# Two of four row groups turned by DMA transposes instead of TensorE, in a spectral-mixing kernel with a feed-forward block

## The chip, the cores and the metric

The kernel runs on one core of a Trainium2 chip. The metric is the time of the program on the device in microseconds (us), as the median of several executions. A core has five engines with a program each: TensorE (PE in the profile; its weight loads are PEld), VectorE (DVE), ScalarE (ACT), GpSimd (POOL) and SyncE (SP). SyncE and GpSimd start the transfers of this kernel.

## The reference

A batch of 8 sequences of 3008 rows with 256 columns is filtered in the frequency domain along the rows, and every filtered row goes through a feed-forward block.

```python
def _attn_ref(x, filt_r, filt_i):               # x: (8, 3008, 256)
    X = np.fft.rfft(x, axis=1)
    F = (filt_r + 1j * filt_i)[None, :, :]
    return np.fft.irfft(X * F, n=x.shape[1], axis=1)

def _moe_ref(x, w_in, w_out, beta):             # x: (24064, 256), w_in: (256, 2048)
    h = x @ w_in
    g = h * (1.0 / (1.0 + np.exp(-beta * h)))
    return g @ w_out
```

## The kernel before

The transform of 3008 = 47 x 64 points is done as small matmuls with tables that the kernel makes itself (t1 to t4), in four parts: over the 47, over the 64 (with the filter product), back over the 64, and back over the 47. Between the parts, what lies in columns must come to lie on partitions, so the data is turned twice. Batch 0 is handled on its own in a prologue; for batches 1 to 7 these parts are units of work that are put among the steps of the feed-forward block. A step is one hidden slice of 128 for one block of 512 rows: two hps matmuls of 512 columns, the Silu on ScalarE (to gT), and, two steps later, four acc matmuls of 256 columns.

In batch 0, the third part writes z_t, with J = 32 rows in four groups of JG = 8:

```python
    z_t = ypool.tile([P, NDC, J, KP], BF16, name="z_t", tag="y")     # NDC 2, KP 96
    ...
    def inverse3(i):                       # i: 0 to 11, two of the 24 frequencies each
        ...
        last = i == NK // 2 - 1
        for j0, j1 in ((0, JG), (JG, J)) if last else ((0, J),):
            ...                            # 8 matmuls into ps, then:
            for e in range(2) if last else (None,):
                ...
                evac(dst, src, not last or j0 > 0)     # evac(dst, src, on_act): a copy out of psum
```

and the turn of a row group is done on TensorE, four rows at a time, with the last part behind it:

```python
    def turn_z(g, i, on_act=False):
        ...
        pz = fpsum.tile([P, 4, D], BF16, name="pz", tag="f")
        for e in range(4):
            for dc in range(NDC):
                nc.tensor.transpose(
                    pz[:KP, e, dc * P : (dc + 1) * P], z_t[:, dc, JG * g + 4 * i + e, :], ident[:]
                )
        evac(zz0[g][:, 4 * i : 4 * i + 4, :], pz[:KP], on_act)

    def last_z(g, i, on_act, own=None):    # four matmuls with zz0[g], and a copy into ys[0]
        ...
```

Group 0 is turned in the prologue by a loop of its own (16 transposes); groups 1 to 3 are placed into steps of the feed-forward block. In batches 1 to 7 the first turn is a DMA transpose from SyncE (a2_read: eight transposes of 128x768, two for each of four groups of six frequencies), the second goes through DRAM (d, zz). `place(a, z, units)` spreads units from step a to step z:

```python
    def uz(g, act=False):
        return [lambda i=i: turn_z(g, i) for i in range(2)] + [
            lambda i=i: last_z(g, i, act) for i in range(2 * NDC)
        ]
    ...
    place(1, 14, uz(1, True))
    place(15, 29, uz(2, True))
    units = uz(3, True)
    place(20, 24, units[:2], per=2)
    place(34, 58, units[2:])
    ...
        at = place(9, 14, units[J // 4 :], per=9)                    # the rest of batch 1's first part
        place(at + 1, at + 1, [lambda: a2_read(1)] + uf(JG, NK), per=9)   # uf: loads of filter rows into frr
        ...
        units = u23(1)                                               # batch 1's second and third parts
        place(20, 53, units[: NK // 2], per=2)
    ...
        place(36, 36, ux(2), per=9)                                  # load of batch 2's rows
        at = place(52, 66, u1(2, True), per=3)
```

The last rows are copied out of psum in two halves, by VectorE and ScalarE, into one tile, which one transfer stores:

```python
                    if last and h == nch - 1:
                        for half in range(2):
                            cols = slice(half * P, (half + 1) * P)
                            evac(ost[:, c : c + per, cols], a[:, :, cols], half == 1)
                    else:
                        evac(ost[:, c : c + per, :], a[:], on_act)
                    store(t0 + h * per * P, per * P, ost[:, c : c + per, :])
```

Of the kernel before, what the change touches and what calls it, by code (L numbers as in the profile page):

```python
# [9 lines left out]
P = 128  # L10
# [3 lines left out]
F32 = mybir.dt.float32  # L14
BF16 = mybir.dt.bfloat16
# [24 lines left out]
def kernel(  # L40
# [66 lines left out]
    def evac(dst, src, on_act, scale=None):  # L107
        if on_act:
            nc.scalar.activation(dst, src, ACT.Copy, scale=1.0 if scale is None else scale)  # L109
        elif scale is None:  # L110
            nc.vector.tensor_copy(dst, src)  # L111
        else:
            nc.vector.tensor_scalar_mul(dst, src, scale)  # L113
# [320 lines left out]
    for go in tabs[::-1]:  # L434
        go()

    z_t = ypool.tile([P, NDC, J, KP], BF16, name="z_t", tag="y")
    pq = {}

    def product(i):  # L440
# [22 lines left out]
    def inverse3(i):  # L463
        k0 = 2 * i
        p_t, q_t = pq.pop(i)

        last = i == NK // 2 - 1
        for j0, j1 in ((0, JG), (JG, J)) if last else ((0, J),):
            nj = 4 * (j1 - j0)
            if j0:  # L470
                ps = fpsum.tile([P, 2, NDC, nj], F32, name="psz", tag="f")
            else:
                ps = opsum.tile([P, 2, NDC, nj], F32, name="psz", tag="acc")
            for src, tab in ((p_t, t3), (q_t, t3b)):
                for e in range(2):
                    for dc in range(NDC):
                        nc.tensor.matmul(  # L477
                            ps[:, e, dc, :],
                            lhsT=src[:, e, dc * P : (dc + 1) * P],
                            rhs=tab[:, k0 + e, 4 * j0 : 4 * j1],  # L480
                            start=src is p_t and dc == 0 and e == 0,
                            stop=src is q_t,
                            skip_group_check=True,
                        )
            for e in range(2) if last else (None,):
                if last:
                    dst = z_t[:, :, j0:j1, 4 * (k0 + e) : 4 * (k0 + e) + 4]
                    src = ps[:, e].rearrange("p c (j a) -> p c j a", a=4)
                else:
                    dst = z_t[:, :, :, 4 * k0 : 4 * k0 + 8].rearrange(  # L490
                        "p c j (e a) -> p e (c j) a", e=2
                    )
                    src = ps.rearrange("p e c (j a) -> p e (c j) a", a=4)
                evac(dst, src, not last or j0 > 0)

    def table4():
        for src, dst in ((t1b, t4b), (t1, t4)):
# [39 lines left out]
    ys[0] = ypool.tile([P, NDC, NK * P], BF16, name="y", tag="y")  # L537
    zz0 = {}
    zz0[0] = apool.tile([P, NK * P], BF16, name="zz", tag="a1")
    zz0[0] = zz0[0][:KP, : JG * D].rearrange("p (j d) -> p j d", j=JG)  # L540


    def turn_z(g, i, on_act=False):
        if g not in zz0:
            zz0[g] = zzpool.tile([KP, JG, D], BF16, name="zz", tag="zz")
        pz = fpsum.tile([P, 4, D], BF16, name="pz", tag="f")
        for e in range(4):
            for dc in range(NDC):
                nc.tensor.transpose(  # L549
                    pz[:KP, e, dc * P : (dc + 1) * P], z_t[:, dc, JG * g + 4 * i + e, :], ident[:]  # L550
                )
        evac(zz0[g][:, 4 * i : 4 * i + 4, :], pz[:KP], on_act)

    def last4(zz, tab, jj, dc, dst, on_act, own=None, first=NP):
        ps = own or fpsum.tile([P, 4, P], F32, name="ps4", tag="f")
        for e in range(4):
            nc.tensor.matmul(  # L557
                ps[:, e, :NP],
                lhsT=zz[:, jj + e, dc * P : (dc + 1) * P],
                rhs=tab[:],  # L560
                start=True,
                stop=True,
            )
        rest = []
        for n0, n1 in ((0, NP),) if own is None or first == NP else ((0, first), (first, NP)):
            rest.append(
                lambda n0=n0, n1=n1: evac(
                    dst[:, n0:n1],
                    ps[:, :, n0:n1].rearrange("p j n -> p n j"),
                    on_act,  # L570
                    inv_scale,
                )
            )
        rest.pop(0)()
        return rest

    def last_z(g, i, on_act, own=None):
        jq, dc = divmod(i, NDC)
        c = g * JG // JC + jq
        yv = ys[0][:, dc, c * CLS : (c + 1) * CLS].rearrange("p (n j) -> p n j", j=JC)  # L580

        n0 = NP if jq == 0 else (TB - CLS) // JC
        return last4(zz0[g], t4b, JC * jq, dc, yv, on_act, own, n0)

    for i in range(4):
        if i % 2:
            pz = opsum.tile([P, 2, D], BF16, name="pz", tag="acc")
        else:
            pz = fpsum.tile([P, 2, D], BF16, name="pz", tag="f")
        for e in range(2):  # L590
            for dc in range(NDC):
                nc.tensor.transpose(
                    pz[:KP, e, dc * P : (dc + 1) * P], z_t[:, dc, 2 * i + e, :], ident[:]
                )
        evac(zz0[0][:, 2 * i : 2 * i + 2, :], pz[:KP], i % 2 == 1)
    pw[0] = hpsum.tile([P, TB], F32, name="pw", tag="hps")
    warm(1)
    rest = []
# [40 lines left out]
            on_act,  # L639
        )  # L640

    def a2_read(b):
        s = st[b]
        s["a2"] = []
        for g in range(NG):
            t = a2pool.tile([P, NDC, KG, P], BF16, name="a2", tag="a2")
            for dc in range(NDC):
                nc.sync.dma_start_transpose(
                    t[:, dc],
                    s["a1"][dc][:, g * KG * P : (g + 1) * KG * P],  # L650
                )
            s["a2"].append(t)

    def s23(b, i):
        s = st[b]
# [38 lines left out]
    def zz_read(b):  # L694
        s = st[b]
        s["zz"] = []
        for h in range(NJG):
            t = zzpool.tile([KP, JG, D], BF16, name="zz", tag="zz")
            nc.sync.dma_start(t[:], s["d2r"][:, h * JG : (h + 1) * JG, :])
            s["zz"].append(t)  # L700

    def s4(b, i, on_act):
# [13 lines left out]
    def place(a, z, units, clear=False, per=1, gap=0):  # L716
        last_at = a
        for n, go in enumerate(units):
            at = a + (z - a) * n / max(1, len(units) - 1)
            at = max(int(at), last_at + gap if n else last_at)  # L720
            if clear and (at % NFB < 2 or at % NFB > 13):
                at += (2 - at) % NFB
            while len(plan.get(at, ())) >= per:
                at += 1
            plan.setdefault(at, []).append(go)
            last_at = at
        return last_at
# [16 lines left out]
        return [lambda i=i: s4(b, i, act and i % 2 == 1) for i in range(J // 2)]  # L744

    def uz(g, act=False):
        return [lambda i=i: turn_z(g, i) for i in range(2)] + [
            lambda i=i: last_z(g, i, act) for i in range(2 * NDC)
        ]

    def uf(a, z):
        return [
# [19 lines left out]
        return [go]  # L772

    place(0, 0, rest, per=9)
    place(1, 14, uz(1, True))
    place(15, 29, uz(2, True))
    units = uz(3, True)
    place(20, 24, units[:2], per=2)
    place(34, 58, units[2:])

    first_step = [(S * b // TB) * NFB for b in range(B + 1)]
    if B > 1:
        units = u1(1, True)
        place(3, 8, units[: J // 4], per=2)
        place(10, 10, uf(0, JG), per=9)
        at = place(9, 14, units[J // 4 :], per=9)
        place(at + 1, at + 1, [lambda: a2_read(1)] + uf(JG, NK), per=9)
        place(14, 20, ut(4), per=2)
        units = u23(1)
        place(20, 53, units[: NK // 2], per=2)  # L790
        at = place(55, 58, units[NK // 2 :], per=2)
        assert at < 60
        place(60, 60, [lambda: zz_read(1)], per=9)
        place(67, 79, u4(1), per=2)
    if B > 2:
        place(36, 36, ux(2), per=9)
        at = place(52, 66, u1(2, True), per=3)
        assert at < 75
        place(75, 75, [lambda: a2_read(2)], per=9)
    for b in range(2, B):  # L800
# [38 lines left out]
    for s in range(len(steps) + LAG):  # L839
# [34 lines left out]
        if s >= LAG:  # L874
# [40 lines left out]
            if fb == NFB - 1:  # L915
                for h, a in enumerate(acc):
                    if h * per % 2 == 0:
                        ost = ostp.tile([P, 2, D], F32, name="ost", tag="ost")
                    c = h * per % 2
                    on_act = h == 0 and i < 6 or last and h == 0  # L920
                    if last and h == nch - 1:
                        for half in range(2):
                            cols = slice(half * P, (half + 1) * P)
                            evac(ost[:, c : c + per, cols], a[:, :, cols], half == 1)
                    else:
                        evac(ost[:, c : c + per, :], a[:], on_act)
                    store(t0 + h * per * P, per * P, ost[:, c : c + per, :])


# [28 lines left out]
```

## Time and profile before

The median of three runs is 776.44 us (775.89 to 776.68). The profiled execution has a span of 775.3 us.

| What | Value |
|---|---|
| TensorE clock granted | full in the whole span |
| acc matmuls in the chain that ended last | 42.4% of the span |
| hps matmuls in that chain | 42.0% |
| first hps matmul of the feed-forward block | at 37.0 us |
| last acc matmuls end, last copies end | 771.6 us, 772.3 us |
| transfers moved | 80.48 MB, mean 104 GB/s |
| the eight DMA transposes of batch 1, on SyncE's queue | from 52.97 us, for 12.04 us |

A page of the profile gives for each engine its busy time, then the span in 40 slices with the busy share of each in tenths, then the chain of work that ended last, and then groups of like instructions: line of the kernel, engine, operation, what it writes and reads with shapes, how often, its busy time in us and the mean of one in ns. A line can be that of a helper (all copies out of psum come from two lines). A timeline has the start in us, the duration, the engine, the line and the operation; like instructions in a row are merged. "SPq" is SyncE's queue: its rows are transfers being issued. The duration of a matmul holds its way through the array, so that neighbours overlap; what one costs is read from start to start.

### The profile page before, as it was taken

Reading aid. Unit: us, or ns where it says so; the run is one execution under the profiler, and the core shown is the slowest. Engines: PE = TensorE matmul, PEld = TensorE weight load, DVE = VectorE, ACT = ScalarE, POOL = GpSimd, SP = SyncE. Lnnn points to the kernel's source line nnn. Section 1 sums busy time; section 2 is a strip of 40 time slices with the busy share of each in tenths; the row PEclk is TensorE's granted clock in tenths of the full one; section 3 lists DMA queues with packets and bytes.
Section 4 is the critical chain, followed back from the end, with each engine's and each line's share of the span. In section 5 each row is a group of like instructions: output and inputs, shape, how many; then the busy total and the mean of one; then the engine's idle time right before and its main releaser. Section 6 shows DMA issues by size and latency. Waiting matters only on the chain.

```text
span 775.3 us, 16219 instructions
## 1 busy us (share of the span) xinstructions
PE 767.5 (99%) x6444; PEld 554.2 (71%) x6444; DVE 379.3 (49%) x641; ACT 594.9 (77%) x926; POOL 142.8 (18%) x145
## 2 busy tenths in 40 slices
PE   8999999999999999999999999999999999999998
PEld 4877777777777777877768777787777776776665
DVE  7836846645446553474526735277353761401001
ACT  6888887886678867788677876778767787677776
POOL 7523401420013100231002410034000430000000
PEclk9999999999999999999999999999999999999999
DMA  7969755515911268022761237512451114100101
GB/s 170 240 164 191 169 164 106 136 55 155 177 43 68 89 145 161 30 85 85 160 134 47 78 116 146 106 64 80 130 110 55 49 69 129 56 28 28 55 28 55
DMA packets 103291, 80.48 MB, mean 104 GB/s; under 512 B 48466, under 2 KB 96996, under 8 KB 102258
## 3 DMA queue, kind: packets, MB, share of 16 engines
q1 hardware_dynamic: 100496, 63.73, 30.8%
q0 software_dynamic: 2720, 15.73, 10.5%
q8 instruction: 50, 0.82, 0.5%
q14 instruction: 25, 0.20, 0.1%
HBM read 46.15 MB, written 35.65 MB: 106 GB/s over the span
## 4 chain that ended last, share of the span: by engine, by line
PE 97%; ACT 1%; DMA 1%; POOL 0%; DVE 0%; issue 0%; POOLq 0%
PE acc L907 42%; PE hps L852 42%; PE ps L557 3%; PE ps L628 2%; PE ps L687 2%; PE ps L661 2%; DMA xg<-in_x_dram 1%; PE psz L477 1%; PE pz L549 0%; ACT a L109 0%; ACT a_t L109 0%; PE pb L403 0%; POOL xg L120 0%; PE ps L451 0%; PE ps2q L451 0%; PE pt L354 0%
## 5 line engine op out<-in xcount | busy, mean ns | idle before, releaser
L867 ACT ACTIVATE gT<-hps,beta_sb 128x512 bf16<-128x512 f32 x752 | 516.0, 688 | 166.8 <-PE hps L852 155.0
L907 PE MATMUL acc<-wout_sb,gT 128*128 128x256 bf16 x3008 | 451.6, 272 | 0.0
L852 PE MATMUL hps<-y,win_sb 128*128 128x512 bf16 (+8 forms) x1730 | 447.7, 351 | 0.0
L907 PEld LDWEIGHTS <-gT 128*128 128x128 bf16 x3008 | 279.6, 98 | 106.3 <-ACT gT L867 0.2
L852 PEld LDWEIGHTS <-win_sb 128*128 128x128 bf16 x1730 | 165.0, 98 | 24.4 <-issue 0.2
L677 POOL TENSOR_TENSOR v_t<-p_t,q_t 128x512 bf16<-128x512 f32 x84 | 106.7, 1270 | 383.9 <-DVE q_t L676 375.4
L111 DVE COPY ost<-acc 128x512 f32<-128x512 f32 (+2 forms) x89 | 56.6, 674 | 194.0 <-PE acc L907 188.4
L111 DVE CAST a<-ps 128x384 bf16<-128x384 f32 x96 | 53.5, 558 | 91.4 <-PE ps L628 91.2
L113 DVE TENSOR_SCALAR y<-ps 128x376 bf16<-128x376 f32 (+1 forms) x115 | 61.7, 544 | 59.5 <-PE ps L557 59.5
L672 DVE TENSOR_TENSOR p_t<-ps,frr 128x512 f32<-128x512 f32 x84 | 58.1, 692 | 33.5 <-PE ps L661 30.9
L676 DVE TENSOR_TENSOR q_t<-ps,fri 64x512 f32<-64x512 f32 x84 | 58.3, 694 | 1.2
L673 DVE SCALAR_TENSOR_TENSOR q_t<-ps,fri 64x512 f32<-64x512 f32 x84 | 57.4, 684 | 1.1
L557 PEld LDWEIGHTS <-zz 96*128 96x128 bf16 x512 | 35.3, 97 | 29.1 <-issue 0.3
L109 ACT ACTIVATE z<-ps 128x512 bf16<-128x512 f32 x84 | 49.6, 590 | 0.0
L628 PEld LDWEIGHTS <-xg 94*128 94x128 bf16 x448 | 30.7, 97 | 23.4 <-issue 0.4
L628 PE MATMUL ps<-t1b,xg 94*128 94x96 bf16 x448 | 36.7, 205 | 0.0
L557 PE MATMUL ps<-t,zz 96*128 96x94 bf16 x448 | 36.7, 204 | 0.0
L687 PE MATMUL ps<-v_t,t 128*128 128x256 bf16 x168 | 32.1, 273 | 0.0
L661 PE MATMUL ps<-a,t 128*128 128x256 bf16 x168 | 32.1, 273 | 0.0
L120 POOL DMA_DIRECT2D xg<-in_x_dram x22 | 12.1, 552 | 97.5 <-PE acc L907 93.9
L661 PEld LDWEIGHTS <-t 128*128 128x128 bf16 x168 | 15.7, 98 | 14.1
L687 PEld LDWEIGHTS <-t 128*128 128x128 bf16 x168 | 16.3, 98 | 6.4 <-DVE q_t L676 0.4
(118 smaller groups left out, 193.9 us busy)
## 6 DMA issues: line engine op xcount, KB each, us to landing
out_dram<-ost SPq DMA_DIRECT2D x80, 256.0 KB
d<-z SPq DMA_DIRECT2D x28, 384.0 KB
zz<-d SPq DMA_DIRECT2D x28, 384.0 KB
xg<-in_x_dram POOLq DMA_DIRECT2D x6, 1280.0 KB, 10.1
frr<-in_filt_r_dram SPq DMA_DIRECT2D x12, 256.0 KB
out_dram<-ost SPq DMA_DIRECT2D x20, 128.0 KB
frr<-in_moe_w_out_dram POOLq DMA_DIRECT2D x4, 512.0 KB, 12.8
xg<-in_x_dram POOLq DMA_DIRECT2D x6, 224.0 KB, 11.0
```

The source lines that it names most:

```text
L111: nc.vector.tensor_copy(dst, src)
L113: nc.vector.tensor_scalar_mul(dst, src, scale)
L557: nc.tensor.matmul(ps[:, e, :NP], lhsT=zz[:, jj + e, dc * P : (dc + 1) * P], rhs=tab[:], start=True, stop=True,)
L628: nc.tensor.matmul(ps[:, e, :KP], lhsT=s["x"][:, 4 * jq + e, dc * P : (dc + 1) * P], rhs=t1b[:], start=True, stop=True,)
L661: nc.tensor.matmul(ps[:, e, :], lhsT=t2[:, k0 + e, 3:5, :].rearrange("p c k -> p (c k)"), rhs=s["a2"][g][:, :, kk + e, :], start=True, sto ...
L672: nc.vector.tensor_tensor(p_t[:], ps[:], frr[:, ks_, :], ALU.mult)
L676: nc.vector.tensor_tensor(q_t[:M], ps[M:P], fri[M:P, ks_, :], ALU.mult)
L677: nc.gpsimd.tensor_tensor(v_t[:], p_t[:], q_t[:], ALU.add)
L687: nc.tensor.matmul(ps[:, e, :], lhsT=t3[:, k0 + e, :], rhs=v_t[:, e, :], start=True, stop=True)
L852: nc.tensor.matmul(hps[:, pos - t0 : pos - t0 + ln], lhsT=win_sb[:, dc, fb * P : (fb + 1) * P], rhs=ys[b][:, dc, n0 : n0 + ln], start=(dc ...
L867: nc.scalar.activation(gT[:, :tn], hps[:, :tn], ACT.Silu, scale=beta_sb[:, fb : fb + 1])
L907: nc.tensor.matmul(acc[tb // per][:, tb % per, :], lhsT=g_[:, tb * P : (tb + 1) * P], rhs=wout_sb[:, f_, :], start=(f_ == 0 and tb % per = ...
```

## The change

Row groups 2 and 3 of batch 0 are no longer turned by TensorE; each is turned by one DMA transpose of 128x2048, so that TensorE and the copies out of psum have less to do. For that z_t gets 128 columns for each row (the last 32 are zeroed on GpSimd) and holds groups 1 to 3; group 0 gets a tile z_0 of its own. The copies of the third part are therefore split in two. The layout of zz is changed in all batches to (column half, row, column). SyncE's queue is reordered: batch 1's transposes, the two new ones and the later filter loads are placed in the order in which they are needed. Batch 2's rows are loaded three steps later, and its first part is placed four steps later. The last two half copies get a tile and a queue each.

```diff
-    z_t = ypool.tile([P, NDC, J, KP], BF16, name="z_t", tag="y")
+    z_0 = a2pool.tile([P, NDC, JG, KP], BF16, name="z_0", tag="a2")
+    z_t = ypool.tile([P, NJG - 1, NDC, JG, P], BF16, name="z_t", tag="y")
+    gp.memset(z_t[:, :, :, :, KP:], 0.0)
 ...
-            for e in range(2) if last else (None,):
-                ...
-                evac(dst, src, not last or j0 > 0)
+            for e0, ne in ((0, 1), (1, 1)) if last else ((0, 2),):
+                cols = slice(4 * (k0 + e0), 4 * (k0 + e0 + ne))
+                if j0 == 0:
+                    evac(z_0[...cols...], ps[...group 0...], not last)
+                if j1 == J:
+                    evac(z_t[...cols...], ps[...groups 1 to 3...], True)
 ...
     def turn_z(g, i, on_act=False):
-        pz = fpsum.tile([P, 4, D], BF16, name="pz", tag="f")
+        pz = fpsum.tile([P, NDC, 4, P], BF16, name="pz", tag="f")
 ...
+    def read_z(g):
+        zz0[g] = zzpool.tile([P, NDC, JG, P], BF16, name="zz", tag="zz")
+        nc.sync.dma_start_transpose(
+            zz0[g].rearrange("p c j d -> p (c j) d"),
+            z_t[:, g - 1].rearrange("p c j r -> p (c j r)"),
+        )
 ...
-            t = zzpool.tile([KP, JG, D], BF16, name="zz", tag="zz")
-            nc.sync.dma_start(t[:], s["d2r"][:, h * JG : (h + 1) * JG, :])
+            t = zzpool.tile([P, NDC, JG, P], BF16, name="zz", tag="zz")
+            t = t[:KP]...                     # seen as (row, column half, column), as before
+            nc.sync.dma_start(t.rearrange("p c j d -> p j c d"), s["d2r"]...)
 ...
-    place(1, 14, uz(1, True))
-    place(15, 29, uz(2, True))
-    units = uz(3, True)
-    place(20, 24, units[:2], per=2)
-    place(34, 58, units[2:])
+    place(1, 14, [lambda i=i: turn_z(1, i, True) for i in range(2)] + uz(1, True))
+    place(23, 30, uz(2, True))
+    place(40, 57, uz(3))
 ...
-        place(at + 1, at + 1, [lambda: a2_read(1)] + uf(JG, NK), per=9)
+        place(at + 1, at + 1, [lambda: a2_read(1, (0,)), lambda: read_z(2)], per=9)
+        place(at + 2, at + 2, [lambda: a2_read(1, (1,))], per=9)
+        place(19, 19, uf(JG, 2 * JG) + [lambda: a2_read(1, (2,))], per=9)
+        place(21, 21, uf(2 * JG, NK) + [lambda: a2_read(1, (3,)), lambda: read_z(3)], per=9)
 ...
-        place(36, 36, ux(2), per=9)
-        at = place(52, 66, u1(2, True), per=3)
+        place(39, 39, ux(2), per=9)
+        at = place(56, 69, u1(2, True), per=3)
 ...
-                        for half in range(2):
+                        for half, eng in ((0, nc.sync), (1, nc.scalar)):
                             cols = slice(half * P, (half + 1) * P)
-                            evac(ost[:, c : c + per, cols], a[:, :, cols], half == 1)
-                    else:
-                        evac(ost[:, c : c + per, :], a[:], on_act)
+                            ost = pqpool.tile([P, 2, D], F32, name="ost", tag="pq"[half] + "_t")
+                            evac(ost[:, :1, :P], a[:, :, cols], half == 1)
+                            eng.dma_start(out[TOK - P :, cols], ost[:, 0, :P])
+                        continue
+                    evac(ost[:, c : c + per, :], a[:], on_act)
                     store(t0 + h * per * P, per * P, ost[:, c : c + per, :])
```

Parts of the diff that only follow the new layouts are cut, and marked with dots. The new uz holds the last_z units alone.

More of the change, by code (lines that the diff above doesn't have):

```diff
@@ L468, in inverse3 @@
         for j0, j1 in ((0, JG), (JG, J)) if last else ((0, J),):
-            nj = 4 * (j1 - j0)
+            ng = (j1 - j0) // JG
             if j0:
-                ps = fpsum.tile([P, 2, NDC, nj], F32, name="psz", tag="f")
+                ps = fpsum.tile([P, 2, ng, NDC, 4 * JG], F32, name="psz", tag="f")
             else:
-                ps = opsum.tile([P, 2, NDC, nj], F32, name="psz", tag="acc")
+                ps = opsum.tile([P, 2, ng, NDC, 4 * JG], F32, name="psz", tag="acc")
             for src, tab in ((p_t, t3), (q_t, t3b)):
@@ L477, in inverse3 @@
                         nc.tensor.matmul(
-                            ps[:, e, dc, :],
+                            ps[:, e, :, dc, :],
                             lhsT=src[:, e, dc * P : (dc + 1) * P],
-                            rhs=tab[:, k0 + e, 4 * j0 : 4 * j1],
+                            rhs=tab[:, k0 + e, 4 * j0 : 4 * j1].rearrange(
+                                "p (g r) -> p g r", g=ng
+                            ),
                             start=src is p_t and dc == 0 and e == 0,
@@ L484, in inverse3 @@
                         )
-            for e in range(2) if last else (None,):
-                if last:
-                    dst = z_t[:, :, j0:j1, 4 * (k0 + e) : 4 * (k0 + e) + 4]
-                    src = ps[:, e].rearrange("p c (j a) -> p c j a", a=4)
-                else:
-                    dst = z_t[:, :, :, 4 * k0 : 4 * k0 + 8].rearrange(
-                        "p c j (e a) -> p e (c j) a", e=2
-                    )
-                    src = ps.rearrange("p e c (j a) -> p e (c j) a", a=4)
-                evac(dst, src, not last or j0 > 0)
+            for e0, ne in ((0, 1), (1, 1)) if last else ((0, 2),):
+                cols = slice(4 * (k0 + e0), 4 * (k0 + e0 + ne))
+                if j0 == 0:
+                    evac(
+                        z_0[:, :, :, cols].rearrange("p c j (e a) -> p e (c j) a", a=4),
+                        ps[:, e0 : e0 + ne, 0].rearrange("p e c (j a) -> p e (c j) a", a=4),
+                        not last,
+                    )
+                if j1 == J:
+                    evac(
+                        z_t[:, :, :, :, cols].rearrange("p g c j (e a) -> p e (g c j) a", a=4),
+                        ps[:, e0 : e0 + ne, (JG - j0) // JG :].rearrange(
+                            "p e g c (j a) -> p e (g c j) a", a=4
+                        ),
+                        True,
+                    )
     def table4():
@@ L539 @@
     zz0[0] = apool.tile([P, NK * P], BF16, name="zz", tag="a1")
-    zz0[0] = zz0[0][:KP, : JG * D].rearrange("p (j d) -> p j d", j=JG)
+    zz0[0] = zz0[0][:, : JG * D].rearrange("p (c j d) -> p c j d", c=NDC, j=JG)
     def turn_z(g, i, on_act=False):
         if g not in zz0:
-            zz0[g] = zzpool.tile([KP, JG, D], BF16, name="zz", tag="zz")
-        pz = fpsum.tile([P, 4, D], BF16, name="pz", tag="f")
[L547 to L552, printed above, removed]
+            zz0[g] = zzpool.tile([P, NDC, JG, P], BF16, name="zz", tag="zz")
+        pz = fpsum.tile([P, NDC, 4, P], BF16, name="pz", tag="f")
+        for dc in range(NDC):
+            for e in range(4):
+                nc.tensor.transpose(pz[:KP, dc, e, :], z_t[:, g - 1, dc, 4 * i + e, :KP], ident[:])
+        evac(zz0[g][:KP, :, 4 * i : 4 * i + 4, :], pz[:KP], on_act)
+    def read_z(g):
+        zz0[g] = zzpool.tile([P, NDC, JG, P], BF16, name="zz", tag="zz")
+        nc.sync.dma_start_transpose(
+            zz0[g].rearrange("p c j d -> p (c j) d"),
+            z_t[:, g - 1].rearrange("p c j r -> p (c j r)"),
+        )
     def last4(zz, tab, jj, dc, dst, on_act, own=None, first=NP):
@@ L558, in last4 @@
                 ps[:, e, :NP],
-                lhsT=zz[:, jj + e, dc * P : (dc + 1) * P],
+                lhsT=zz[:KP, dc, jj + e, :],
                 rhs=tab[:],
@@ L586 @@
         if i % 2:
-            pz = opsum.tile([P, 2, D], BF16, name="pz", tag="acc")
+            pz = opsum.tile([P, NDC, 2, P], BF16, name="pz", tag="acc")
         else:
-            pz = fpsum.tile([P, 2, D], BF16, name="pz", tag="f")
+            pz = fpsum.tile([P, NDC, 2, P], BF16, name="pz", tag="f")
         for e in range(2):
             for dc in range(NDC):
[L592 to L595, printed above, removed]
+                nc.tensor.transpose(pz[:KP, dc, e, :], z_0[:, dc, 2 * i + e, :], ident[:])
+        evac(zz0[0][:KP, :, 2 * i : 2 * i + 2, :], pz[:KP], i % 2 == 1)
     pw[0] = hpsum.tile([P, TB], F32, name="pw", tag="hps")
@@ L640, in s1, with a2_read @@
         )
-    def a2_read(b):
+    def a2_read(b, gs=range(NG)):
         s = st[b]
-        s["a2"] = []
-        for g in range(NG):
+        for g in gs:
             t = a2pool.tile([P, NDC, KG, P], BF16, name="a2", tag="a2")
@@ L651, in a2_read @@
                 )
-            s["a2"].append(t)
+            s.setdefault("a2", []).append(t)
     def s23(b, i):
@@ L697, in zz_read @@
         for h in range(NJG):
-            t = zzpool.tile([KP, JG, D], BF16, name="zz", tag="zz")
-            nc.sync.dma_start(t[:], s["d2r"][:, h * JG : (h + 1) * JG, :])
+            t = zzpool.tile([P, NDC, JG, P], BF16, name="zz", tag="zz")
+            t = t[:KP].rearrange("p c j d -> p (c j d)").rearrange("p (j c d) -> p c j d", c=NDC, j=JG)
+            nc.sync.dma_start(
+                t.rearrange("p c j d -> p j c d"),
+                s["d2r"][:, h * JG : (h + 1) * JG, :].rearrange("r j (c d) -> r j c d", c=NDC),
+            )
             s["zz"].append(t)
@@ L746, in uz @@
     def uz(g, act=False):
-        return [lambda i=i: turn_z(g, i) for i in range(2)] + [
-            lambda i=i: last_z(g, i, act) for i in range(2 * NDC)
-        ]
+        return [lambda i=i: last_z(g, i, act) for i in range(2 * NDC)]
     def uf(a, z):
@@ L921 @@
                     if last and h == nch - 1:
-                        for half in range(2):
+                        for half, eng in ((0, nc.sync), (1, nc.scalar)):
                             cols = slice(half * P, (half + 1) * P)
-                            evac(ost[:, c : c + per, cols], a[:, :, cols], half == 1)
-                    else:
-                        evac(ost[:, c : c + per, :], a[:], on_act)
+                            ost = pqpool.tile([P, 2, D], F32, name="ost", tag="pq"[half] + "_t")
[3 more added lines that the diff above has]
+                    evac(ost[:, c : c + per, :], a[:], on_act)
                     store(t0 + h * per * P, per * P, ost[:, c : c + per, :])
```

## The prediction

> **What bounds the kernel now.** I read the page from the top: the engines' busy times, the chain that ended last, the groups of instructions, and then the timeline of TensorE, of ScalarE and VectorE before 37 us, of SyncE's queue between 50 and 80 us, and of the last six microseconds.
>
> ```profile
> PE 767.5 (99%) x6444; PEld 554.2 (71%) x6444; DVE 379.3 (49%) x641; ACT 594.9 (77%) x926; POOL 142.8 (18%) x145
> PE   8999999999999999999999999999999999999998
> ...
> PE 97%; ACT 1%; DMA 1%; POOL 0%; DVE 0%; issue 0%; POOLq 0%
> ```
>
> TensorE is 97% of the chain. The other engines have room on average, so what is taken off them alone brings nothing. But a busy TensorE in a trace need not be at its peak, so I compared the starts of its groups in the timeline with the time that their columns need:
>
> ```profile
> 53.83 0.59 PE L852 MATMUL hps<-y,win_sb 128*128 128x512 bf16 x2
> 54.26 0.61 PE L549 MATMUL pz<-ident,z_t 128*96 128x128 bf16 x8
> 54.71 0.60 PE L907 MATMUL acc<-wout_sb,gT 128*128 128x256 bf16 x4
> 55.15 0.59 PE L852 MATMUL hps<-y,win_sb 128*128 128x512 bf16 x2
> ```
>
> Start to start, two matmuls of 512 columns take 0.43 us, four of 256 take 0.44 us, and eight transposes of 128 columns take 0.45 us, or 56 ns each. The same holds from 37 us to 769 us: going through all groups of that stretch in this way, I find single pauses of 0.1 to 0.2 us (at 38.8, 46.8, 82.8 and 97.0 us) and no others worth naming. TensorE waits for nothing else there. So a microsecond of columns removed is a microsecond of time, and nothing else done between 37 and 769 us can gain more than those pauses.
>
> Outside that stretch lie two short ones: the prologue up to 37 us, and the tail from the last matmul (771.6 us) to 775.3 us. In the prologue VectorE and ScalarE pace one another:
>
> ```profile
> 23.37 0.68 DVE L460 TENSOR_TENSOR pb_t<-ps,fri 128x512 bf16<-128x512 f32 x1
> 23.97 0.68 DVE L460 TENSOR_TENSOR qb_t<-ps2q,fri 128x512 bf16<-128x512 f32 x1
> 24.56 0.68 DVE L460 TENSOR_TENSOR pb_t<-ps,fri 128x512 bf16<-128x512 f32 x1
> ```
>
> ```profile
> 22.91 0.59 ACT L109 ACTIVATE z_t<-psz 128x512 bf16<-128x512 f32 x1
> 23.42 0.81 ACT L109 ACTIVATE a<-pb 128x768 bf16<-128x768 bf16 x1
> 24.12 0.59 ACT L109 ACTIVATE z_t<-psz 128x512 bf16<-128x512 f32 x1
> ```
>
> A step of two frequencies costs VectorE 2 x 0.60 = 1.20 us from start to start, and ScalarE 0.70 + 0.51 = 1.21 us. Both run without a gap from 22.2 to about 26.6 us; after 30 us ScalarE has pauses of 0.5 us and only VectorE stays full, up to 33.9 us.
>
> **What the Trainium skill says.** "TensorE: Matmul & The Clock Gate", Part 1 ("Wait — 56ns, not 53.3ns?"), gives a warm matmul of N columns N / 2.4 GHz plus about 2.5 ns; the trace agrees (56 ns for 128). "DMA: Bandwidth & Descriptors", "Anatomy of one DMA", says that DMA engines don't wait on semaphores and the issuing sequencer does: so SyncE's queue is served in program order, and a store stuck there holds up the transposes behind it. The same page, "Silent corruption: two transposing streams in flight at once", wants all transposes of a time in one stream; the change keeps to SyncE, and its price is just that order. "PSUM — Partial Sum Buffer", in its table of terms, calls a simultaneous access of two engines to one bank a collision, reads included. The tail agrees: ScalarE's half of the last copy starts only when VectorE's half of the same accumulator is done.
>
> **Part by part.**
>
> 1. *Transposes of row groups 2 and 3 leave TensorE.* Each group is 8 rows x 2 column halves = 16 transposes. The group of instructions (three row groups in it) is
>
> ```profile
> L549 PE MATMUL pz<-ident,z_t 128*96 128x128 bf16 x48 | 3.7, 219 | 0.0
> ```
>
> The 219 ns are latency in the pipeline; the share in the chain is 56 ns each. Removed are 32: 32 x 0.056 = 1.79 us, all on the path. Group 1 keeps its 16, group 0 its 16 (its psum layout changes, not its count).
>
> 2. *Copies of these transposes.* Four VectorE copies of 0.69 us (54.9 to 66.3 us) vanish: off the path, worth 0. Group 1's two copies go from VectorE to ScalarE, about 1.0 us each there by my estimate (its copies of 192 and 512 columns took 0.328 and 0.594 us, which makes 0.17 fixed and 0.83 ns for a column, so 1024 take 0.17 + 0.85). They fall into steps 1 and 3, at 38 to 42 us, where ScalarE has a pause of 1.38 us before 41.9. TensorE's two hps buffers give it some 1.7 us from one use to the next; 1.0 + 0.7 is at that edge. I set +0.1 us.
>
> 3. *Splitting the copies of the prologue.* Eleven ScalarE copies of 512 columns become 128 + 384. From 328 ns for 192 columns and 594 for 512, an extra instruction costs 0.08 to 0.1 us of ScalarE. In the seven steps where ScalarE is full that is 0.6 to 0.7 us, less the few tenths of pause there; TensorE runs 0.9 us ahead of VectorE's products, so most of it is swallowed, and the end of VectorE's row of products hardly moves. In return the first turn of group 0 no longer waits for a whole z_t copy (0.06 us). I set +0.1 us. The memset on GpSimd lies in its 1.57 us of waiting for the filter at 20.8 to 22.4 us: 0.
>
> 4. *The two DMA transposes and the queue.* In the kernel before:
>
> ```profile
> 52.97 12.04 SPq L648 DMA_TRANSPOSE a<-a  x8
> ...
> 69.07 10.42 SPq L826 DMA_DIRECT2D out_dram<-ost  x10
> ```
>
> One transpose of 128x768 (six blocks of 128) holds the queue for 1.21 to 1.3 us, so one of 128x2048 (16 blocks) should hold it for about 3.3 us and land within a microsecond more. First, for group 2: batch 1's group 0 takes 53.0 to 55.6, then z to 58.9, landed near 60 us. It is wanted in step 23, which starts at 62.7 us before and near 61.3 us with the transposes gone: it fits, with 1 us. Then, for group 3: batch 1's second read to 61.5; ten stores, 0.45 us each if the rings are free (4.5 to 5 us); four filter loads (1.8); two transposes (2.6); four filter loads (1.8); two transposes (2.6); z (3.3): 78.4 to 79.5, landed near 80 us. It is wanted in step 40, at 81.0 us before and near 79.0 us after. This is a dead heat: TensorE may wait 0 to 2 us. I set +0.3 us, as the change starts its last_z only at 40 (34 before) and puts batch 2's load behind it, which looks like a fit to such a landing.
>
> 5. *Filter loads in two parts.* Rows 8 to 15 are wanted in step 32 (72.2 us before, near 70.5 after) and would land near 71 us. VectorE may wait for a moment; the inverse runs three units behind, so TensorE shouldn't. 0.
>
> 6. *The tail.* The two halves of the last copy get their own tiles and their own queues, but still read one psum bank, so they should stay one after the other (771.65 and 771.98 us). The first half's store starts 0.3 us sooner, the second is half as large and follows its copy on ScalarE itself. I set -0.1 us.
>
> Later batches: the read of zz is only a relabelling with the same contiguous rows, and the loads at 39 and 56 are the same work; 0.
>
> Sum: -1.79 + 0.1 + 0.1 + 0.3 - 0.1 = -1.4 us, so 776.44 - 1.4 = about 775.0 us.
>
> **Rivals.** (a) *Everything hidden*: only the columns and the tail count, -1.9 us, 774.5 us; for it speaks that TensorE met no wait worth naming for any DMA before. (b) *The transposed group 3 arrives late*: the wait for zz takes the place of the removed transposes. The queue of before speaks for it (ten stores held it for 10.42 us[...]; such a hold again would bring z to 85 us and cost TensorE 5 us, 778 to 780 us). Against it speaks that those stores now come before the filter loads. A wait of 1 to 2 us gives 775.5 to 776.5 us, no gain. (c) *The prologue becomes ScalarE's*: if the 0.7 us goes through whole, 775.4 us. (d) *The transposes slow other transfers*: stores and batch 2's rows have slack of tens of microseconds; little.
>
> **Range and chances.** (a) gets 45%, a short wait or a lengthened prologue 40%, a full loss 15%. So 775.0 us, and eight times in ten between 773.9 and 776.7 us; the three runs before lie 0.8 us apart. Two per cent is 15.5 us: all that leaves TensorE is 1.8 us, so faster by over 2% is out of reach, and slower by over 2% would need a stall in every batch.
>
> **What would show it.** Right: the transposes of pz from z_t in the feed-forward fall from 48 to 16, the step rhythm stays (0.43 and 0.44 us), and the first hps matmul of step 0 stays within 0.3 us of 37.0 us. Step 4 is shown by what the first group-3 matmul at step 40 waits for: nothing (a), or DMA zz (b). Step 2 by pauses of hps between 38 and 43 us. Step 6 by whether the two last copies overlap. The prediction is wrong if hps in the later blocks comes less than 1 us or more than 2 us earlier than before, or if a new wait stands at 61 or 80 us.

## The result, and the profile after

The changed kernel takes 783.12 us (median, 781.45 to 784.3) against 776.16 us for the kernel before: a ratio of 1.0087, 95% interval 1.0072 to 1.0102. It is slower by some 7 us, where 775.0 us was predicted.

The page of the changed kernel, engines and chain:

```profile
PE 768.1 (98%) x6412; PEld 553.6 (71%) x6412; DVE 377.3 (48%) x639; ACT 595.4 (76%) x935; POOL 144.1 (18%) x146
...
PE 94%; DMA 2%; ACT 1%; SPq 1%; issue 0%; DVE 0%; POOL 0%; ACTq 0%; DVEq 0%; POOLq 0%
```

TensorE has 32 matmuls less, as the change meant. Yet it fills only 94% of the chain (97% before). DMA has twice its share, and SyncE's queue has come in, which the chain didn't have. The transposes that are left (groups by shape):

```profile
L560 PE MATMUL pz<-ident,z_t 128*96 128x128 bf16 x16 | 1.2, 219 | 0.0
```

They are 16 instead of 48, each as long as before. So the columns went, and waits came. The timeline of TensorE from step 39 on (in brackets: what ended an idle time):

```profile
78.22 0.59 PE L869 MATMUL hps<-y,win_sb 128*128 128x512 bf16 x2
82.88 0.50 PE L573 MATMUL ps<-t4b,zz 96*128 96x94 bf16 x4 [4.06 <-DMA zz<-z_t]
83.17 1.06 PE L924 MATMUL acc<-wout_sb,gT 128*128 128x256 bf16 x4
84.02 1.06 PE L869 MATMUL hps<-y,win_sb 128*128 128x512 bf16 x2
...
94.78 0.60 PE L924 MATMUL acc<-wout_sb,gT 128*128 128x256 bf16 x4
96.84 0.59 PE L869 MATMUL hps<-y,win_sb 128*128 128x512 bf16 x2 [1.46 <-ACT gT L884]
```

Three losses stand in these lines. At step 40 TensorE stops for 4.06 us until group 3's DMA transpose has landed. Behind that stop the same matmuls take twice as long from start to start: 0.85 us for two of 512 columns instead of 0.43. And in step 50 an hps matmul waits 1.46 us for ScalarE. The second is seen in a table by stage (busy time of PE, PEld, DVE, ACT and POOL, then the granted clock, the DMA share and GB/s):

```profile
80.00:82.00 2.00, 0.00 (x0) 0.00 (x0) 0.00 (x0) 0.00 (x0) 2.00 (x3) 0.76 1.37 94
82.00:84.00 2.00, 1.12 (x8) 0.90 (x9) 0.55 (x1) 0.00 (x0) 0.02 (x1) 0.50 1.50 271
84.00:86.00 2.00, 2.00 (x10) 1.12 (x8) 0.39 (x1) 0.71 (x2) 0.00 (x0) 0.50 0.69 132
88.00:90.00 2.00, 2.00 (x17) 1.42 (x15) 0.13 (x1) 1.46 (x3) 1.15 (x1) 1.00 1.21 200
```

From about 81 to 88 us the clock is 0.50. In the third row TensorE counts as fully busy and gets through 10 matmuls; in the last it gets through 17. The Trainium skill has this in "TensorE: Matmul & The Clock Gate", Part 1: TensorE falls to half its clock after an idle window of about 3.4 us. In this trace a stop of 4.06 us is followed by half the clock, and one of 1.46 us is not. But in e2 below a stop of 2.40 us is followed by it too, so a shorter stop than the page gives can be enough.

The third loss has a longer story. SyncE's queue and ScalarE's copies in the same trace, and the load of batch 2's rows on GpSimd's queue:

```profile
75.11 4.23 SPq L565 DMA_TRANSPOSE zz<-z_t  x1
79.45 4.52 SPq L843 DMA_DIRECT2D out_dram<-ost  x5
84.06 7.13 SPq L705 DMA_DIRECT2D d<-z  x2
```

```profile
80.92 1.10 POOL L120 DMA_DIRECT2D xg<-in_x_dram  x2
95.61 0.60 ACT L109 ACTIVATE z<-ps 128x512 bf16<-128x512 f32 x1 [2.06 <-DMA d<-z]
```

The first write of d is issued at 84.06 us, three microseconds after the load of the rows. It lands near 95.5 us. Until then its z tile is taken; there are two, so the copy to the third z (batch 1, unit 9, step 47) waits, and the gT behind it on ScalarE starts only at 96.11 us. In the kernel before, the order was the reverse:

```profile
79.58 7.49 SPq L692 DMA_DIRECT2D d<-z  x2
...
81.73 1.10 POOL L120 DMA_DIRECT2D xg<-in_x_dram  x2
```

What the order means is shown by the transfers of each queue (packets, MB, share; q1 is SyncE's, q0 GpSimd's). First the changed kernel, 84 to 86 us; then the kernel before, 80 to 82 and 82 to 84 us:

```profile
q0 software_dynamic: 16, 0.26, 68.8%
q1 hardware_dynamic: 1, 0.00, 0.2%
```

```profile
q1 hardware_dynamic: 288, 0.52, 67.5%
...
q0 software_dynamic: 15, 0.25, 91.7%
```

In both traces the transfer issued first gets through first. A packet of the load has 16 KB (0.26 MB in 16), one of SyncE's 1.8 KB (0.52 MB in 288). While the load runs, SyncE's queue moves next to nothing. The Trainium skill says, in "DMA: Bandwidth & Descriptors", "Queues, rings and completion order", that a DMA engine takes the queues in turn, packet by packet. With one such packet in each turn SyncE would have a tenth of the bytes, by an estimate from these sizes; measured from 84 to 90 us were 0.04 MB in 35 packets beside 1.03 MB in 63. So turns of one packet each don't explain the share; what does stays open.

The sum of the two profiled executions, in us: columns -1.79 (32 x 0.056); first hps at 36.69 instead of 37.00, -0.31; from the last matmul to the end 3.55 instead of 3.67, -0.12; step 40, +4.23; half the clock, +2.4 (what the groups from 82.88 to 87.43 us take beyond their columns); step 50, +1.62. That makes +6.0, and the spans differ by 6.0 (781.3 and 775.3).

### The profile page after: what moved, and what is told of

Its sections match the earlier page's. It is cut to its first block, busy times and chain, and to the rows that moved or that the text cites. A ratio compares the mean times of both kernels' runs of the same rounds, so it can differ in the third digit from the quotient of the medians.

```text
span 781.3 us, 16163 instructions
## 1 busy us (share of the span) xinstructions
PE 768.1 (98%) x6412; PEld 553.6 (71%) x6412; DVE 377.3 (48%) x639; ACT 595.4 (76%) x935; POOL 144.1 (18%) x146
## 4 chain that ended last, share of the span: by engine, by line
PE 94%; DMA 2%; ACT 1%; SPq 1%; issue 0%; DVE 0%; POOL 0%; ACTq 0%; DVEq 0%; POOLq 0%
PE acc L924 42%; PE hps L869 41%; PE ps L573 3%; PE ps L642 2%; PE ps L674 2%; PE ps L700 2%; DMA d<-z 1%; DMA xg<-in_x_dram 1%; PE psz L480 1%; SPq L843 1%; ACT a L109 0%; ACT a_t L109 0%; PE pb L403 0%; POOL xg L120 0%; ACT gT L884 0%
## 5 line engine op out<-in xcount | busy, mean ns | idle before, releaser
L113 DVE TENSOR_SCALAR y<-ps 128x376 bf16<-128x376 f32 (+1 forms) x119 | 63.9, 544 | 64.0 <-PE ps L573 64.0
```

## The experiments

Theory A is the simple one: group 3's transpose lands too late for step 40, and all else follows from that stop. Theory B: SyncE's whole queue is late behind the new transposes, and as it falls behind the load of batch 2's rows it starves; each buffer that waits for something on that queue can then stop TensorE. All runs are edits of the changed kernel unless said otherwise; a ratio is to the kernel before on the same chip.

| Run | us | ratio | 95% interval |
|---|---|---|---|
| changed kernel | 783.12 | 1.0087 | 1.0072 to 1.0102 |
| e1 late group 3 | 785.17 | 1.0107 | 1.0092 to 1.0122 |
| e2 late rows (step 48) | 786.91 | 1.0136 | 1.0118 to 1.0154 |
| e3 both | 779.09 | 1.0027 | 1.0017 to 1.0038 |
| e4 group 3 on TensorE | 775.98 | 0.9991 | 0.9984 to 0.9998 |
| e5 rows in step 45 | 781.37 | 1.0064 | 1.0049 to 1.0079 |
| e8 e5, wait filled | 780.73 | 1.0052 | 1.0035 to 1.0069 |
| e7 late group 3, rows in step 45 | 775.17 | 0.9981 | 0.9974 to 0.9987 |
| e6 group 3's transpose early, rows in step 45 | 776.71 | 0.9999 | 0.9993 to 1.0006 |
| e11 group 3's transpose early | 775.71 | 0.9991 | 0.9983 to 0.9999 |
| e12 e1 with a third z tile | 780.87 | 1.0043 | 1.0027 to 1.0059 |
| e9 kernel before with the new tail | 776.28 | 1.0000 | 0.9992 to 1.0009 |
| e10 without DMA transposes of z | 776.61 | 1.0001 | 0.9993 to 1.0009 |

**e1: group 3 wanted later.**

```diff
-    place(40, 57, uz(3))
+    place(48, 58, uz(3))
```

> Group 3's last part starts in step 48 instead of 40; nothing else differs from the changed kernel. Theory A (the late landing of group 3's transpose, near 82.7 us, is the whole loss, with the halved clock behind it): no wait is left, 774.3 to 775.3 us. Theory B (SyncE's queue as a whole is late: the first write of d is issued at 84 us behind group 3's transpose and then starves beside the load of batch 2's rows, landing near 92 to 95 us): TensorE now reaches step 47 near 87 us, ScalarE's copy to z waits there for d until 92 to 95 us, and the time taken out at step 40 comes back: 779 to 783 us.

Measured 785.17 us, beyond even theory B's range. The stop at step 40 is gone, and the one behind step 47's copy has grown (timeline):

```profile
88.06 0.60 PE L924 MATMUL acc<-wout_sb,gT 128*128 128x256 bf16 x4
95.43 0.60 ACT L109 ACTIVATE z<-ps 128x512 bf16<-128x512 f32 x1 [8.77 <-DMA d<-z]
96.66 1.01 PE L869 MATMUL hps<-y,win_sb 128*128 128x512 bf16 x2 [8.00 <-ACT gT L884]
```

d still lands near 95.4 us; TensorE arrives sooner, waits the longer, and again pays with half the clock (the last line takes 1.01 us). Theory A falls: the stop at step 40 had hidden most of the other.

**e2 and e3: the load of rows out of the way.**

```diff
-        place(39, 39, ux(2), per=9)
-        at = place(56, 69, u1(2, True), per=3)
+        place(48, 48, ux(2), per=9)
+        at = place(60, 72, u1(2, True), per=3)
```

e2 has this edit alone, e3 has it with that of e1.

> Batch 2's rows are loaded in step 48 instead of 39 (their first part from step 60 instead of 56); group 3 as in the changed kernel. Theory A: the wait of 4 us at step 40 and the halved clock stay, and so does the later wait, as it is a consequence: 782 to 784 us. Theory B: the wait at step 40 stays, but d's write no longer meets the load, lands within 4 us, and the wait of 1.6 us near 95 us goes: 781 to 782 us.

> Both of the above. Theory A: no more than with the late group 3 alone, the two within 0.5 us. Theory B: this alone takes both waits away: 774.0 to 775.0 us, 4 us or more below the run with the late group 3 alone, and below the kernel before by 1.2 to 2.2 us.

In both, the wait of the z copy for d is gone, as theory B said. But the times miss: I had put the load too late for its own readers. In e3 batch 2's first part waits 3.15 us for its rows, and the half clock follows; in e2 it waits 2.40 us, besides the stop at step 40, and the half clock follows there too (timeline and table of e2):

```profile
108.53 0.80 PE L642 MATMUL ps<-t1b,xg 94*128 94x96 bf16 x8 [2.40 <-DMA xg<-in_x_dram]
109.00:110.00 1.00, 1.00 (x10) 0.73 (x8) 0.56 (x1) 0.49 (x1) 0.00 (x0) 0.50 0.80 311
```

Without its new stop, of 3.3 us from start to start, and some 1.8 us at half clock, e3 would have been near 774 us. That is an estimate; e7 runs it.

**e4: group 3 back on TensorE.**

```diff
+    place(20, 24, [lambda i=i: turn_z(3, i) for i in range(2)], per=2)
-        ..., lambda: a2_read(1, (3,)), lambda: read_z(3)], per=9)
+        ..., lambda: a2_read(1, (3,))], per=9)
```

> Group 3 is turned by TensorE again (16 transposes in steps 20 and 24 as before), group 2 by DMA; places as in the changed kernel. The queue is shorter by the 4.2 us of one transpose. Theory A: only group 3's transpose was at fault, so half of the columns' gain is left: 775.0 to 775.5 us. Theory B: d's first write is issued near 80 us, at the same time as the load of batch 2's rows in step 39, and may starve in part: 775 to 779 us, with a wait of ScalarE's z copy for d near step 47 if it does.

775.98 us, above theory A's range and in theory B's, 0.6 us below the kernel before on its chip, and TensorE has no stop in the trace. d is issued at 80.88 us, the load at 81.99 us. So the order held by one microsecond, in step 39 too; the load is no harm where SyncE is first.

**e5 and e8: only the stop at step 40, and that stop with work in it.** Batch 2's rows are loaded in step 45, their first part from step 63 (e5). e8 adds, ahead of group 3's first part:

```diff
+        for _ in range(16):                  # nothing uses the result
+            nc.tensor.matmul(ps..., lhsT=ident[:], rhs=win_sb[:, 0, :TB], start=True, stop=True)
```

> The changed kernel with batch 2's rows loaded in step 45 (39) and their first part from step 63 (56), so that the rows are there in time, as they were not in the run with step 48. Theory B: what is left is the wait for group 3 at step 40, 4.2 us, and its halved clock, 2.1 us, no wait for d and none for the rows: 780.0 to 781.0 us. Theory A (the wait of ScalarE's z copy near 95 us follows from the stall at step 40): it stays, 782 to 784 us.

> As the run before, with 16 matmuls of 512 columns put into step 40 ahead of group 3's first part; they compute nothing that is used and take 16 x 0.216 = 3.45 us, less than the wait there. If the halved clock after the wait is a loss of its own, caused by TensorE's idling, it goes although the wait lasts as long: 2 us below the run before, 778.0 to 779.0 us. If the clock falls for another reason, or the half clock costs nothing beside other waits, the time stays at 780 to 781 us.

e5: 781.37 us, a little above its range, with the stop of 4.05 us at step 40 and no wait for d or rows. The wait for d came from the load and not from the stop, which theory A had said. e8: the 16 matmuls fill the stop up to a last 0.52 us, and the clock stays full. The same stage in e5 and then in e8:

```profile
84.00:86.00 2.00, 2.00 (x10) 1.13 (x8) 1.96 (x3) 0.79 (x2) 0.00 (x0) 0.50 0.34 135
```

```profile
84.00:86.00 2.00, 2.00 (x19) 1.54 (x19) 1.12 (x2) 0.80 (x2) 0.00 (x0) 1.00 0.70 260
```

So idling costs the clock. From the end of the stop to group 3's next matmuls e5 takes 7.07 us (82.20 to 89.27) and e8 5.39 us (83.90 to 89.29): in these traces the half clock costs 1.7 us, near the 2 us expected. Both spans are 778.9 us all the same, because e8's execution came to the end of the stop 1.7 us later: its first hps matmul started 0.65 us later, and at 47 us TensorE waited 0.96 us for batch 1's rows, both ahead of the edit. The medians differ by 0.6 us and not by 2, with intervals that overlap, and e8's lies in the range of the other reading; so the gain is shown for this stretch and not for the whole run.

**e7: both waits out of the way.** e1's edit, and the rows as in e5.

> Group 3's last part from step 48 (40) and batch 2's rows in step 45, their first part from step 63. Theory B: both waits go and no other comes: 774.0 to 775.0 us, 1.5 to 2.3 us below the kernel before. If the queue still brings something late, it is d for step 47 (issued near 83 us, wanted near 87 us): up to 777 us.

775.17 us, just above the range, and 0.9981 (0.9974 to 0.9987): faster than the kernel before by 1.5 us, the lowest ratio of all, and close to the 1.79 us of the columns. TensorE has no stop of more than 0.3 us in the feed-forward. Group 3's transpose and five stores still stand ahead of d on SyncE's queue, as in e1; what has changed is that d comes before the load (timeline):

```profile
83.30 1.04 SPq L705 DMA_DIRECT2D d<-z  x2
86.33 1.10 POOL L120 DMA_DIRECT2D xg<-in_x_dram  x2
```

**e6 and e11: group 3's transpose early.** It is issued in step 16, behind batch 1's second read. e11 has this edit alone; e6 has the rows in step 45 too.

```diff
-        place(at + 2, at + 2, [lambda: a2_read(1, (1,))], per=9)
+        place(at + 2, at + 2, [lambda: a2_read(1, (1,)), lambda: read_z(3)], per=9)
```

> Group 3's transpose is issued right behind group 2's and batch 1's second (step 16 instead of 21), with group 3's last part from step 40 as in the changed kernel, and batch 2's rows in step 45. Theory B: the transpose takes 1.6 us of the queue instead of 4.2, lands near 63 us, d is issued near 81 us; no wait: 774.0 to 775.0 us. A rival: the filter rows for units 4 to 11 come 1.6 us later and VectorE holds up the second part: 775 to 777 us.

> The changed kernel with group 3's transpose in step 16 (21) and nothing else moved, so batch 2's rows are loaded in step 39 as in the changed kernel. Theory A (the landing of group 3's transpose is the loss): 774.5 to 776.7 us, as it lands near 63 us. Theory B: d's first write is issued near 82 us, just behind the load of rows, lands only when that is through, near 92 us or later, and TensorE is held at step 47, near 87 us, by ScalarE's copy to z: 780 to 785 us.

e11 came out at 775.71 us, where I had expected 780 to 785 by theory B. I had taken d to be issued behind the load; in the trace it is ahead of it (81.20 and 82.91 us). d comes 2.9 us sooner than in the changed kernel, as the early transpose holds the queue for 1.68 us instead of 4.23; and the load comes 2.0 us later, as it stands on GpSimd behind products that wait for VectorE. The theory stands, its premise didn't hold here, and the second half of that was luck. This run alone doesn't part the theories; e1 and e5 do. The price of the early transpose is the rival named for e6: the filter rows come later, and VectorE waits for them (timeline of e11):

```profile
74.10 0.69 DVE L685 TENSOR_TENSOR p_t<-ps,frr 128x512 f32<-128x512 f32 x1 [4.03 <-DMA frr<-in_filt_r_dram]
```

Six microseconds later VectorE's backlog stops TensorE for 1.0 us in e11, and in e6 for as long (776.71 us, in the rival's range).

**e12: a third z tile.** With e1's edit, the first z tile of batch 1 lies in a free slot of another pool. This takes away the buffer's wait and leaves the starved queue.

```diff
-                s["z"] = zpool.tile([P, KG, D], BF16, name="z", tag="z")
+                own = b == 1 and g == 0
+                s["z"] = (a2pool if own else zpool).tile(..., tag="a2" if own else "z")
```

> As the run with the late group 3 alone (785.17 us, with a wait of 8.8 us of ScalarE's z copy for d), but the first z tile of batch 1 lies in a slot of the a2 pool that is free then, so three z tiles are there instead of two. Batch 2's rows are still loaded in step 39, and d is still issued behind them. Theory B with the buffer as the link (d's write stays late, near 92 to 96 us, but nothing waits for its tile): the waits go, 774.5 to 776.5 us. If the late write of d holds TensorE up in another way, or the load itself slows what TensorE needs: 778 to 785 us.

780.87 us, in single runs from 775.04 to 783.51 us. The wait for d is gone, and the next buffer on the same queue takes its place (timeline):

```profile
93.66 0.69 DVE L111 COPY ost<-acc 128x512 f32<-128x512 f32 x1 [5.21 <-DMA out_dram<-ost]
96.53 0.61 PE L703 MATMUL ps<-v_t,t 128*128 128x256 bf16 x2 [4.45 <-DVE q_t L689]
```

VectorE waits for an output tile whose store, issued at 80.4 us, hangs behind the load; the filter products stand behind that copy, and TensorE behind them. So z's buffer was one link among several, and the starved queue is the cause. Four of the 20 runs stayed below 777 us; what spared them isn't shown, as the trace is of a run of 781.97 us.

**e9 and e10: tail and layout alone.** e9 is the kernel before with the new last stores. e10 is the changed kernel with all z transposes on TensorE, and with the places, queue and loads of before.

> The kernel before with the new tail alone: the two last half copies in tiles of their own, one stored from SyncE, one from ScalarE. From the changed kernel's trace, in which the time from the last matmul to the end of the span fell from 3.65 to 3.45 us: 0.1 to 0.3 us below the kernel before. The two halves still come one after the other, as both read one psum bank. If the halves were kept apart by their tile, ScalarE's would start 0.3 us sooner and the gain would be 0.4 to 0.6 us.

> The changed kernel without both DMA transposes: TensorE turns groups 2 and 3 as before, in the places of before, with the queue and the loads in the order of before; new stay the layouts, the split copies of the prologue, the memset, group 1's copies on ScalarE, and the tail. If the split copies and the memset lengthen the prologue: 776.5 to 777.5 us, above the kernel before. If they are swallowed, as the changed kernel's trace with its first hps matmul 0.3 us sooner suggests: 0 to 0.5 us below the kernel before.

Neither differs from the kernel before: 1.0000 and 1.0001, both within 0.0009 (0.7 us). In e9 the two halves still come one after the other, ScalarE's 1.21 us after its last work and just behind VectorE's. The gain of 0.2 us that e9's expectation reads from the changed kernel's trace is smaller there (3.55 us from the last matmul to the end, 3.67 before), and e9's own trace shows none (3.69 us).

## Why the prediction was wrong

- *Step 1, the columns*: right. 16 transposes are left, and e7 keeps 1.5 of the 1.79 us.
- *Steps 2 and 3, the copies and the prologue*: I had set +0.1 us each; e10 finds nothing, within 0.7 us. The trace shows no pause of hps between 38 and 43 us beyond that of before, and the first hps matmul comes 0.31 us sooner, about the 0.3 that were named and within the scatter of the other traces (36.0 to 37.0 us).
- *Step 4, the queue*: this is the step that failed. Its landing "within a microsecond more" was 3.4 us: the queue let go of z at 79.34 us, and the tile was there at 82.7. It was wanted "near 79.0 us", and in fact at 78.7. So "TensorE may wait 0 to 2 us. I set +0.3" was 4.2 us, and the sign that was named came, a new wait at 80 us.
- *The queue's sum in step 4*: that "78.4 to 79.5" holds 79.34 is luck. Its terms add up to 78.1 to 78.6, and their errors cancel: a hold of 3.3 us was set for both new transposes, and group 2's took 1.59 and group 3's 4.23 (5.51 in e12). "1.21 to 1.3 us" for a transpose of 128x768 leaves out one of the eight, which took 2.27 us; the line shown, 12.04 us for eight, makes 1.5 us each with the pauses. What sets the hold stays open. Transposes in front are not enough: e11's early one follows two of batch 1's and group 2's, and takes 1.68 us. Only the late one has filter rows among the entries shortly ahead of it; no run tests whether they are the reason.
- *The fit in step 4*: that a start at step 40 "looks like a fit to such a landing" was no evidence; it showed where the part had been placed, not when the tile would land.
- *What a stop costs besides its length* wasn't in the sum: 2.4 us at half the clock in the changed kernel's trace, 1.7 us in e5's.
- *Rival (d)*, "stores and batch 2's rows have slack of tens of microseconds; little", was the second error. I looked at what the transposes' transfers do to others, and not at what SyncE's queue holds back behind them: d's first write, wanted by a tile of which there are two, went from ahead of the load of batch 2's rows to behind it. e1 shows 8.8 us of ScalarE's wait and 8.0 us of TensorE's from that alone.
- *Step 5*: VectorE does wait for filter rows, and where it is short TensorE doesn't mind (e5, e3: 2.3 and 2.5 us); where it is 4.0 us (e11), TensorE loses 1.0 us.
- *Step 6, the tail*: one after the other, as said; the gain of 0.1 us is not seen in e9.
- *Range*: 776.7 us as its upper end left out rival (b)'s own 778 to 780 us, which came nearest to what happened.

## What to carry to other kernels

Before work is moved from a full engine to a queue that is served in order, list everything behind the new entry on that queue, what buffer each holds, how many there are and when the next one is wanted; then see which large transfer on another queue it will now come after. Taking one wait away shows only the next one on the same queue (e1, e12), so repair the order and not the wait. And where the gain is 1.8 us, a transfer that lands as a dead heat can turn it into a loss: a stop long enough to drop the clock costs more than its length.

## What was unexpected in the hardware

- Group 3's transposed tile, when it is late, moves with a gap of some 1.3 us, in which 0 to 10 GB/s flow (about 80.3 to 81.6 us in the changed kernel); the last part lands after that gap. Around group 2's tile, and around the early one in e11, the gaps are 0.5 to 0.8 us, and inside a burst 270 to 300 GB/s flow. What causes them is open.
- A load in packets of 16 KB leaves another queue with packets of 1.8 KB about 4% of the bytes for 6 us (0.04 of 1.07 MB).
- In these traces, from step 0 of the feed-forward on, the clock is halved after every stop of 2.4 us or more and after none of 1.5 us or less. The half clock begins 2.2 to 5.3 us after the start of the stop, in e3 and e5 when TensorE is at work again, and it lasts about 3.4 us (e3, e5, the later one in e2) or about 6.8 us (the changed kernel, e1, e12). With idle matmuls in the stop (e8) it doesn't come.
